# Two dense layers over pairs of token blocks: eight weight groups run upwards and downwards in turn

## The chip, the cores and the metric

One core of one Trainium2 chip runs the whole program in one launch. The metric is the device time of that launch in microseconds (us); a kernel's time is the median of several runs. A profiled execution is one more run, with its own time.

## The reference, cut to what matters

```python
qn = q / (norm(q, axis=1) + 1e-6); kn = k / (norm(k, axis=1) + 1e-6)
a = softmax(kn.T @ qn / tau)                # 256 x 256
x = v @ a                                   # 6016 tokens x 256
h = x @ w_in;  g = h * clip(h + 3, 0, 6) / 6;  x = g @ w_out      # first layer, 256 -> 2048 -> 256
h = maximum(x @ w_in2, 0);  out = (h * h) @ w_out2                # second layer, the same sizes
```

All in float32. The softmax over channels comes first and is short; the kernel multiplies its result into `w_in`, so that the first layer starts from `v` itself.

## The kernel before, in words

Everything is held with channels on the 128 partitions and tokens along the free dimension. Every float32 operand of a product is split into a high and a low part, and each product of two operands is three matmuls (high by high, low by high, high by low).

*Pairs and groups.* The 6016 tokens are cut into six pairs of blocks: five pairs of 2 x 512 tokens and one of 2 x 448 (`pairs`, `NP` = 6). The 2048 hidden channels are cut into eight groups of 256 (`NG` = 8). The list `groups` says in which order the work goes: layer, then pair, then group, groups 0 to 7 in each pair, 96 entries in all. The loop at line 2026 walks over it; `i` is the place in the list and `k = i - K0` the place within the second layer (`K0` = 48). I call the place of a group within its pair its *position*; before the change position and group number are the same.

*A group of the second layer* (`first7s`, `second_of`). A pair of blocks and a group form a 2 x 2 by 2 x 2 block product, which is done with seven products instead of eight. The seven products of the first matrix go through two PSUM banks, X and Y (tile xy, lines 1659 to 1661); ACT copies a bank out (L1671), VectorE adds (L1677), ACT squares or applies the ReLU (L1684), and the split into high (ACT, L1690) and low (VectorE, L1695) follows. The four blocks of a group stand in the tile pairs named rs, rp, hs and rc in turn: groups 0 and 4 in rs, 1 and 5 in rp, 2 and 6 in hs, 3 and 7 in rc. The second matrix takes seven products as well (lines 1802 to 1804, into acc, B, C and xy), three of which need sums of the blocks. These sums are made by DMA: a *move* is an accumulating DMA from SBUF to SBUF that POOL issues (L1711). Each group has two: the first adds one tile to two others (512 KB, `chain`), the second, which waits for the first, adds one to one (256 KB, `chain4`). Three groups later (`LAG`) TensorE uses what they made; ACT and VectorE split it before (`split_t`).

*Weights.* The first matrix of a group, with its sums already formed, lies in DRAM (`w1_d`) and is loaded by SP in two halves of 448 KB (L595, tile w, three buffers `WB` in a ring), two groups ahead (`load_w1(*groups[i + 2])`). In the second layer the first half of group `i + 2` waits until the first move of group `k - 2` has landed, and the second half until its second move has. The second matrix stays in SBUF.

*Other transfers on SP's queue.* SP issues in program order. The tokens of the next pair come in four parts of 256 KB (L817, tile xr), one for each group from position 0 on; with the fifth step of the generator `tokens` the differences of the tokens and their splits are put in (L836 and on). The four results of a pair (`finish_a` at position 0, `finish_b` at position 2 of the next pair) are put into a list `pending`, from which one store is issued per group (L1898).

*What sets the order.* TensorE and the DMA queues take their work in program order. For VectorE, ACT and POOL a planner (`Plan`) takes the operations by due times from a list of costs, tries this 200 times with shifted ranks and emits the best order. So a change in what is asked for, or in when, can change the order of all three engines at other places too.

The lines that the change touches: `w1_tile`, `load_w1`, `fold` and `fold2` (buffers of the weights), `second` (first and last group of an accumulation), `groups`, `by7` and `fast`, `first7s` (choice of the tile pair) and the main loop.

Of the kernel before, what the change touches and what calls it, by code (L numbers as in the profile page):

```python
# [19 lines left out]
P = 128  # L20
# [176 lines left out]
def tile_kernel(  # L197
# [59 lines left out]
    SOME = ()  # L257
    GAP = 2

    PSUM = bass.MemoryType.PSUM  # L260
# [8 lines left out]
    op8_p = ctx.enter_context(tc.tile_pool(name="op8", bufs=2))  # L269
    w1_p = ctx.enter_context(tc.tile_pool(name="w1", bufs=WB))  # L270
    dram = ctx.enter_context(tc.tile_pool(name="dram", bufs=1, space=bass.MemoryType.DRAM))
# [258 lines left out]


    OPW = {"a21": 0, "a11": 1, "a22": 2, "a12": 3, "s1": 4, "s2": 5, "s3": 6, "s4": 7}
    op8_r, w1_r = Ring(2), Ring(WB)
    w1, w1_done, w1_held = {}, {}, {}
# [32 lines left out]

    def w1_tile():
        return pools["w1"].tile([P, 2, 7, P], F32R, tag="w1", name="w1")

# [12 lines left out]
    def load_w1(l, pr, g):  # L583
        p = {}
        a, b = (0, 4) if plain(l, pr) else (1, 8)

        w1[l, pr, g] = p
        free = w1_r.take()
        w1_done[l, pr, g], w1_held[l, pr, g] = [], w1_r.last

        def part(h, waits=()):
            def f():
                if not h:
                    p["w"] = w1_tile()
                o.ins = nc.sync.dma_start(p["w"][:, h, : b - a].bitcast(F32), w1_d[l, g][:, h, a:b])  # L595
                for x in waits:
                    tc.add_manual_dep(
                        o.ins.ins, x.ins.ins.name,
                        mybir.DependencyInfo(mybir.DependencyClass.Sync, mybir.DependencyReason.DATA),
                        reason="order",  # L600
                    )

            o = add("DMA", 0.15 * (b - a), f, free, list(w1_stored[l, g]), *waits, lat=1.5)
            w1_done[l, pr, g].append(o)

        return part
# [6 lines left out]
    def fold(g):  # L613
# [8 lines left out]
        taken, op8_held = op8_r.take(), op8_r.last  # L622
        w1_taken, held = w1_r.take(), w1_r.last
        w1[0, 0, g], w1_done[0, 0, g], w1_held[0, 0, g] = w, [], held
# [8 lines left out]
        for k, es in enumerate(halves):  # L633
# [27 lines left out]
            def place(a=a, b=b):  # L661
                if a == 0:
                    w["w"] = w1_tile()
                return w["w"][:, 0, a:b], w["w"][:, 1, a:b]
# [17 lines left out]
    def fold2(fb):  # L682
# [3 lines left out]
        ts, ws = [{}, {}], [{}, {}]  # L686
        taken, op8_held, w1_taken, held, evs = [], [], [], [], [[], []]
        for k, g in enumerate(gs):
            taken.append(op8_r.take())
            op8_held.append(op8_r.last)  # L690
        for k, g in enumerate(gs):
            w1_taken.append(w1_r.take())
            held.append(w1_r.last)
            w1[0, 0, g], w1_done[0, 0, g], w1_held[0, 0, g] = ws[k], [], held[k]
# [27 lines left out]
        for k, g in enumerate(gs):  # L722

            def place(k=k):
                ws[k]["w"] = w1_tile()
                return ws[k]["w"][:, 0, 0:4], ws[k]["w"][:, 1, 0:4]

            p, ops = split_w(ts[k], 0, 4, place, evs[k], op8_held[k], w1_taken[k])
            w1_done[0, 0, g].extend(ops)

            def f_st(k=k, g=g):
                nc.sync.dma_start(a_d[g], ts[k]["op8"][:, 0:4])

            def store(k=k, g=g, p=p, ops=ops, f_st=f_st):
                a_stored[g] = add("DMA", 0.73, f_st, evs[k], lat=1.5)
                op8_held[k].append(a_stored[g])
                held[k].append(store_w1(0, g, 0, 4, p, ops))

            stores.append(store)
# [672 lines left out]
    def second(l, pr, g, out):  # L1412

        n = pairs[pr][1]
        for k, (b, i) in enumerate(TILES):
            t, half, gh, gl, held = out[k]
            first_of, last_of_b = g == 0 and k in (0, 2), g == NG - 1 and k in (1, 3)
            free = [acc_r[b, e].take() for e in range(NC)] if first_of else [(), ()]
# [82 lines left out]

    groups = [(l, pr, g) for l in range(2) for pr in range(NP) for g in range(NG)]
    K0 = groups.index(FIRST)
    LAG = 3

    def by7(l, pr, g):
        if groups.index((l, pr, g)) < K0:
            return False
        return g in SOME if l == 0 else pr < NP - 1 or g < NG - 2

    def fast(l, pr):
        return groups.index((l, pr, 0)) >= K0

# [128 lines left out]
    def first7s(l, pr, g):  # L1642
# [3 lines left out]
        seven = by7(l, pr, g)  # L1646
        A2, B2 = cells["R"][g % 4]
        R = A2.part + B2.part
# [377 lines left out]
    for i, (l, pr, g) in enumerate(groups):  # L2026
# [13 lines left out]
        elif i >= len(groups) - 2 and us[k - 2]["seven"]:  # L2040
            us[k - 2]["chain4"]()
        for _ in range(1 if k >= 0 else len(pending)):
            if pending and len(us) - pending[0][0] >= HOLD:
# [7 lines left out]
        if l == 0 and pr == 0:  # L2051
            if g + 1 < NG:
# [3 lines left out]
                if g % 2 == 1 and g + 3 < NG:  # L2056
                    need_win((g + 3) // 2)
        if g == (0 if l else 2) and i + NG < len(groups):
            x_load = tokens(*groups[i + NG][:2], k >= 0)
            if k < 0:  # L2060
                list(x_load)
        if k >= 0 and i + NG < len(groups):
            next(x_load, None)
        if k == -5:
# [9 lines left out]
        if k >= 0:  # L2074
# [31 lines left out]
            if k + 1 in due:  # L2106
                us[due[k + 1]]["split_t"]()
            if k and g == 0:
                finish_a(NP * l + pr - 1)
            if k >= NG and g == 2:  # L2110
                finish_b(NP * l + pr - 1)
# [72 lines left out]
```

## Time and profile before

| | |
|---|---|
| median of 3 runs | 1027.7 us (1026.87 to 1028.27) |
| profiled execution | 1026.52 us, of which the span from the first to the last instruction is 1024.7 |
| TensorE busy | 1006.7 us, 98% of the span |
| VectorE, ACT, POOL busy | 908.3, 796.3, 139.4 us |
| mean granted clock of TensorE | 0.998 |
| bytes moved | 199.24 MB |

In the profile PE is TensorE's matmul, PEld its weight load (a little ahead of PE), DVE VectorE, ACT ScalarE, POOL GpSimd, SP the engine that issues most DMAs (SPq its queue). "<-" in a wait names what ended it; `x2` counts merged instructions, and then the duration reaches from the first to the end of the last, with what lies between. The granted clock is in parts of full speed (1.00 is 2.4 GHz, 0.50 is 1.2). The first layer's matmuls end at about 548 us; the second layer runs from there to the end.

### The profile page before, as it was taken

The page shows a single profiled execution, that of the slowest core. Times are in us where ns is not written, and L with a number is a line of the kernel's source. Part 1 is how long each engine was busy: PE and PEld are TensorE (multiplying, and loading weights), DVE is VectorE, ACT ScalarE, POOL GpSimd, SP SyncE. Part 2 cuts the span into 40 slices and gives each one's busy share as a digit, 9 for nine tenths or more (in the row PEclk, how much of TensorE's full clock was granted, in tenths as well). Part 3 has the DMA queues.
Part 4 walks back from the last instruction along what each step waited for, and adds up shares of the span by engine and source line. Part 5 has one row for each costly group of instructions (what it writes and reads, how often), then busy time and mean ns, then how long its engine had stood idle before and what let it go on. Part 6 is the DMA issues. An engine that isn't in the chain of part 4 may idle for free.

```text
span 1024.7 us, 13075 instructions
## 1 busy us (share of the span) xinstructions
PE 1006.7 (98%) x4484; PEld 838.6 (82%) x4484; DVE 908.3 (89%) x1388; ACT 796.3 (78%) x1213; POOL 139.4 (14%) x153
## 2 busy tenths in 40 slices
PE   9999999999999999999999989999999999998998
PEld 8888888888888888888998868788888778787897
DVE  4899988888999999999899979998998888897886
ACT  6787667677778678778768879889889779787884
POOL 4300010000000000010000211222222212122221
PEclk9999999999999999999999999999999999999999
DMA  9657527545445556555764977978989878797883
GB/s 373 253 175 246 180 105 249 176 143 181 151 182 171 195 177 198 185 185 157 263 207 161 231 171 181 219 192 209 226 196 210 202 178 190 176 232 156 204 216 76
DMA packets 73075, 199.24 MB, mean 194 GB/s; under 512 B 7728, under 2 KB 12080, under 8 KB 71856
## 3 DMA queue, kind: packets, MB, share of 16 engines
q1 hardware_dynamic: 49872, 146.63, 43.2%
q0 software_dynamic: 22848, 51.32, 24.5%
q8 instruction: 35, 0.57, 0.2%
q10 hardware_dynamic: 288, 0.46, 0.1%
q14 instruction: 32, 0.26, 0.1%
HBM read 128.45 MB, written 34.34 MB: 159 GB/s over the span
## 4 chain that ended last, share of the span: by engine, by line
PE 67%; DMA 16%; issue 7%; DVE 5%; ACT 3%; POOL 2%; SPq 0%; DVEq 0%; POOLq 0%; ACTq 0%
PE acc L1430 8%; PE acc L1429 8%; PE acc L1435 8%; DMA rs<-rs 6%; DMA hs<-hs 3%; PE xy L1659 3%; PE A L1336 3%; PE A L1337 3%; PE A L1338 3%; PE xy L1661 3%; PE xy L1660 3%; DMA qk<-in_qk_dram 3%; DMA rc<-rc 3%; DMA rp<-rp 2%; PE B L1338 2%
## 5 line engine op out<-in xcount | busy, mean ns | idle before, releaser
L1429 PE MATMUL acc<-g,wo 128*128 128x512 f32 (+1 forms) x384 | 148.2, 386 | 0.0
L1430 PE MATMUL acc<-g,wo 128*128 128x512 f32 (+1 forms) x384 | 148.2, 386 | 0.0
L1218 ACT ACTIVATE g<-r 128x1024 fp32r<-128x1024 f32 (+1 forms) x96 | 100.1, 1043 | 48.2 <-DVE r L1192 47.9
L1222 DVE TENSOR_TENSOR g<-r,g 128x1024 fp32r<-128x1024 f32 (+1 forms) x96 | 115.4, 1202 | 12.0 <-ACT g L1218 11.9
L1435 PE MATMUL acc<-g,wo 128*128 128x512 f32 (+1 forms) x384 | 116.9, 386 | 0.0
L1659 PE MATMUL xy<-xt,w 128*128 128x512 f32 (+1 forms) x192 | 76.0, 396 | 8.7 <-ACT hs L1671 6.0
L1435 PEld LDWEIGHTS acc<-g,wo 128*128 128x128 f32 x384 | 72.1, 188 | 13.8
L1429 PEld LDWEIGHTS acc<-g,wo 128*128 128x128 f32 x384 | 72.1, 188 | 13.7
L1430 PEld LDWEIGHTS acc<-g,wo 128*128 128x128 f32 x384 | 72.1, 188 | 13.6
L1661 PE MATMUL xy<-xt,w 128*128 128x512 f32 (+1 forms) x192 | 74.5, 388 | 0.0
L1660 PE MATMUL xy<-xt,w 128*128 128x512 f32 (+1 forms) x192 | 74.4, 388 | 0.0
L1187 ACT ACTIVATE r<-hp,three 128x1024 f32<-128x1024 f32 (+1 forms) x40 | 45.3, 1132 | 34.8 <-DVE hp L1369 34.4
L1695 DVE TENSOR_TENSOR gs<-rs,gs 128x512 fp32r<-128x512 f32 (+3 forms) x60 | 52.5, 883 | 11.2 <-ACT gs L1690 11.1
L1690 ACT ACTIVATE gs<-rs 128x512 fp32r<-128x512 f32 (+3 forms) x60 | 47.0, 786 | 16.5 <-DMA rs<-rs 15.3
L1659 PE MATMUL xy<-xb,w 128*128 128x512 f32 (+1 forms) x144 | 56.7, 393 | 1.8 <-ACT hs L1684 0.7
L1695 DVE TENSOR_TENSOR gs<-hs,gs 128x512 fp32r<-128x512 f32 (+3 forms) x58 | 50.9, 884 | 6.8 <-ACT gs L1690 6.7
L1802 PE MATMUL acc<-gs,wo 128*128 128x512 f32 (+1 forms) x146 | 56.4, 386 | 0.0
L1804 PE MATMUL acc<-gs,wo 128*128 128x512 f32 (+1 forms) x146 | 56.3, 386 | 0.0
L1803 PE MATMUL acc<-gs,wo 128*128 128x512 f32 (+1 forms) x146 | 56.3, 385 | 0.0
L1661 PE MATMUL xy<-xb,w 128*128 128x512 f32 (+1 forms) x144 | 55.6, 386 | 0.0
L1660 PE MATMUL xy<-xb,w 128*128 128x512 f32 (+1 forms) x144 | 55.6, 386 | 0.0
L1695 DVE TENSOR_TENSOR gs<-rp,gs 128x512 fp32r<-128x512 f32 (+3 forms) x60 | 52.9, 882 | 1.9 <-ACT gs L1690 1.7
(393 smaller groups left out, 2850.4 us busy)
## 6 DMA issues: line engine op xcount, KB each, us to landing
w<-w1d SPq DMA_DIRECT2D x176, 448.0 KB, 4.5
qk<-in_qk_dram SPq DMA_DIRECT2D x8, 1024.0 KB, 14.8
w1d<-wA POOLq DMA_DIRECT2D x16, 448.0 KB, 3.8
xr<-in_vT_dram SPq DMA_DIRECT2D x5, 1024.0 KB, 7.4
x2d<-o SPq DMA_DIRECT2D x20, 256.0 KB, 5.0
rs<-rs POOLq DMA_DIRECT2D x10, 512.0 KB, 8.3
rp<-rp POOLq DMA_DIRECT2D x10, 512.0 KB, 6.5
hs<-hs POOLq DMA_DIRECT2D x10, 512.0 KB, 6.5
```

Source lines behind the costliest of these rows:

```text
L1218: A.activation(t["g"][:, a:b, 0, :n], t["t"][:, a:b, :n], AF.Copy)
L1222: V.tensor_tensor(g[:, a:b, 1, :n], t["t"][:, a:b, :n], g[:, a:b, 0, :n].bitcast(F32), ALU.subtract)
L1429: T_.matmul(acc[b, e][:, :n], w(e, 0), gh_, start=first_of, stop=False)
L1430: T_.matmul(acc[b, e][:, :n], w(e, 1), gh_, start=False, stop=False)
L1435: T_.matmul(acc[b, e][:, :n], w(e, 0), gl_, start=False, stop=last_of_b)
L1659: T_.matmul(ps, wh, xh, start=start, stop=False, skip_group_check=True)
L1660: T_.matmul(ps, wl, xh, start=False, stop=False, skip_group_check=True)
L1661: T_.matmul(ps, wh, xl, start=False, stop=True, skip_group_check=True)
L1695: V.tensor_tensor(lo, src.ap()[..., :n], h.bitcast(F32), ALU.subtract)
L1802: T_.matmul(ps, wh, gh, start=first, stop=False, skip_group_check=True)
L1803: T_.matmul(ps, wl, gh, start=False, stop=False, skip_group_check=True)
L1804: T_.matmul(ps, wh, gl, start=False, stop=last, skip_group_check=True)
```

## The change

1. `groups` runs the eight groups of a pair downwards in some pairs: in the first layer in pairs 2 and 4, in the second in pairs 1, 3 and 5.
2. Each weight buffer has a name of its own, and `Slots` decides ahead of time which group lies in which of the three. A group whose weights are still there is *kept*: `load_w1` then issues nothing. So the first three groups of a pair that turns back are not loaded: four times in the first layer and five times in the second.
3. In the second layer the stores in `pending` are issued at positions 2, 5, 6 and 7 (`POPS`), one each, from the layer's second pair on; in its first pair all that are ready are issued at once. The four token parts come at positions 0 (two), 1 and 2, and the differences with the step at position 3 (`PARTS`).
4. What was said by group number (first and last of an accumulation, tile pair, the ends of a pair) is now said by position.

```diff
+    POPS = {2: 1, 5: 1, 6: 1, 7: 1}
+    PARTS = {0: 2, 1: 1, 2: 1, 3: 1}
...
-    w1_p = ctx.enter_context(tc.tile_pool(name="w1", bufs=WB))
+    w1_p = ctx.enter_context(tc.tile_pool(name="w1", bufs=1))
...
+    groups = []
+    for l in range(2):
+        for pr in range(NP):
+            back = pr % 2 if l else pr > 1 and pr % 2 == 0
+            groups += [(l, pr, g) for g in (reversed(range(NG)) if back else range(NG))]
+    K0 = groups.index(FIRST)
+    at_of = {key: i % NG for i, key in enumerate(groups)}
+
+    class Slots:
+        def __init__(self):
+            now, used = [None] * WB, [-WB + i for i in range(WB)]
+            self.of, self.kept = {}, set()
+            for i, (l, pr, g) in enumerate(groups):
+                what = (l, g, l == 0 and pr < PLAIN)
+                if what in now:
+                    self.kept.add((l, pr, g))
+                    k = now.index(what)
+                else:
+                    k = used.index(min(used))
+                now[k], used[k] = what, i
+                self.of[l, pr, g] = k
+            self.held, self.has = [[] for _ in range(WB)], [None] * WB
+
+        def take(self, key):
+            k = self.of[key]
+            free, self.held[k], self.has[k] = self.held[k], [], key
+            return free, self.held[k], k
...
     def load_w1(l, pr, g):
-        p = {}
+        p, key = {}, (l, pr, g)
         a, b = (0, 4) if plain(l, pr) else (1, 8)
-
-        w1[l, pr, g] = p
-        free = w1_r.take()
-        w1_done[l, pr, g], w1_held[l, pr, g] = [], w1_r.last
+        if key in w1_s.kept:
+            was = w1_s.has[w1_s.of[key]]
+            w1_s.has[w1_s.of[key]] = key
+            for of in w1, w1_done, w1_held:
+                of[key] = of[was]
+            return lambda *_: None
+
+        w1[key] = p
+        free, held, slot = w1_s.take(key)
+        w1_done[key], w1_held[key] = [], held
...
-            first_of, last_of_b = g == 0 and k in (0, 2), g == NG - 1 and k in (1, 3)
+            at = at_of[l, pr, g]
+            first_of, last_of_b = at == 0 and k in (0, 2), at == NG - 1 and k in (1, 3)
...
-    groups = [(l, pr, g) for l in range(2) for pr in range(NP) for g in range(NG)]
-    K0 = groups.index(FIRST)
...
-        return g in SOME if l == 0 else pr < NP - 1 or g < NG - 2
+        return g in SOME if l == 0 else (l, pr, g) not in groups[-2:]
...
-        A2, B2 = cells["R"][g % 4]
+        A2, B2 = cells["R"][at_of[l, pr, g] % 4]
...
-        for _ in range(1 if k >= 0 else len(pending)):
+        pos = i % NG
+        for _ in range(POPS.get(pos, 0) if k >= NG else len(pending)):
             if pending and len(us) - pending[0][0] >= HOLD:
                 pending.pop(0)[1]()
...
-        if g == (0 if l else 2) and i + NG < len(groups):
+        if pos == (0 if l else 2) and i + NG < len(groups):
...
         if k >= 0 and i + NG < len(groups):
-            next(x_load, None)
+            for _ in range(PARTS.get(pos, 0)):
+                next(x_load, None)
...
-            if k and g == 0:
+            if k and pos == 0:
                 finish_a(NP * l + pr - 1)
-            if k >= NG and g == 2:
+            if k >= NG and pos == 2:
                 finish_b(NP * l + pr - 1)
```

The change moves instructions at other places too, through the planner. TensorE's rows are the same in the same order, but for line numbers. Three places, where "group" counts positions within the pair:

POOL, pair 1 of the second layer, the moves of groups 2 (hs), 3 (rc) and of group 4 (rs); 128x2x512 is a group's first move, 128x512 its second. Before:

```order
L1711 DMA hs_5109<-hs_5122 128x2x512
L1711 DMA hs_5122<-hs_5109 128x512
L1711 DMA rc_5186<-rc_5204 128x2x512
L1711 DMA rc_5204<-rc_5186 128x512
L1711 DMA rs_4950<-rs_4975 128x2x512
L1711 DMA rs_4975<-rs_4950 128x512
```

The same moves after the change:

```order
L1746 DMA hs_5062<-hs_5075 128x2x512
L1746 DMA rc_5139<-rc_5157 128x2x512
L1746 DMA hs_5075<-hs_5062 128x512
L1746 DMA rc_5157<-rc_5139 128x512
L1746 DMA rs_4905<-rs_4924 128x2x512
L1746 DMA rs_4924<-rs_4905 128x512
```

The second move of hs has gone behind the first of rc. It stands so at groups 2 and 3 of pairs 0, 3, 4 and 5 before, and of all six pairs after; at groups 0 and 1 of pairs 0, 2, 3 and 4 before, and of pairs 2, 3 and 4 after (and of groups 4 and 5 of pair 5 only before).

SP, pair 3 of the second layer; w is a group's two halves (x2), xr a part of the next pair's tokens, out_dram a store. Positions 0 to 5 before:

```order
L595 DMA w_6803<-w1d_119 128x896 x2
L817 DMA xr_6861<-x2d_137 128x512
L595 DMA w_6878<-w1d_120 128x896 x2
L817 DMA xr_6861<-x2d_137 128x512
L595 DMA w_6960<-w1d_121 128x896 x2
L1898 DMA out_dram<-c_6849 128x512
L817 DMA xr_6861<-x2d_137 128x512
L595 DMA w_7033<-w1d_122 128x896 x2
L817 DMA xr_6861<-x2d_137 128x512
L595 DMA w_7110<-w1d_123 128x896 x2
L1898 DMA out_dram<-c_6863 128x512
L595 DMA w_7178<-w1d_124 128x896 x2
```

Positions 0 to 7 after, where the pair runs downwards:

```order
L853 DMA xr_6737<-x2d_137 128x512 x2
L631 DMA w_6816<-w1d_121 128x896 x2
L853 DMA xr_6737<-x2d_137 128x512
L631 DMA w_6898<-w1d_120 128x896 x2
L1933 DMA out_dram<-c_6790 128x512
L853 DMA xr_6737<-x2d_137 128x512
L631 DMA w_6971<-w1d_119 128x896 x2
L631 DMA w_7048<-w1d_118 128x896 x2
L631 DMA w_7109<-w1d_117 128x896 x2
L1933 DMA out_dram<-c_6801 128x512
L1933 DMA out_dram<-c_6917 128x512
L1933 DMA out_dram<-c_6951 128x512
```

At position 0 the weights have gone and two token parts stand there; the token part of position 3 and the store of position 4 have gone from their places; at positions 6 and 7, where before two groups of weights and two stores follow, only stores are left.

VectorE, pair 3, group 3 and the beginning of group 4; c is a result of the pair before, xt the first difference of the next pair's tokens (xr), f a running sum. Before:

```order
L1677 ISA rc<-xy,rc 128x512
L1923 TENSOR_TENSOR c_6863<-c_6863,f_5104 128x512
L1839 TENSOR_TENSOR f_5712<-xy,f_5712 128x512
L1695 TENSOR_TENSOR gs<-rc,gs 128x512
L1767 TENSOR_TENSOR rc<-rc 128x512
L1677 ISA rs<-xy,rs 128x512
L1695 TENSOR_TENSOR gs<-rc,gs 128x2x512
L1695 TENSOR_TENSOR gs<-rp,gs 128x512
L1695 TENSOR_TENSOR gs<-rc,gs 128x512
L1677 ISA rs<-xy,rs 128x512 x2
L1695 TENSOR_TENSOR gs<-hs,gs 128x2x512
L836 TENSOR_TENSOR xt_7127<-xr_6861 128x512
```

After:

```order
L1712 ISA rc<-xy,rc 128x512
L872 TENSOR_TENSOR xt_6995<-xr_6737 128x512
L1874 TENSOR_TENSOR f_5668<-xy,f_5668 128x512
L1730 TENSOR_TENSOR gs<-rc,gs 128x512
L1802 TENSOR_TENSOR rc<-rc 128x512
L1712 ISA rs<-xy,rs 128x512
```

The difference xt stands ten rows earlier, in the place of c; that row of c stands near the end of group 5 now.

## Rows read from the trace of the kernel before

**Rows 1.** Windows, first layer: us, busy us (instructions) by engine, clock, DMA.

```profile
75.00:525.00 450.00, 450.00 (x2007) 376.54 (x2006) 413.89 (x645) 334.19 (x475) 21.81 (x39) 1.00 0.55 187
```

**Rows 2.** Windows, the six pairs of the second layer, columns as in rows 1.

```profile
546.40:624.50 78.10, 74.70 (x323) 59.30 (x323) 67.71 (x107) 65.06 (x105) 13.80 (x13) 1.00 0.76 188
624.50:702.00 77.50, 77.27 (x337) 62.60 (x336) 69.95 (x99) 66.42 (x104) 17.00 (x16) 1.00 0.85 204
702.00:778.30 76.30, 76.30 (x337) 62.77 (x336) 70.40 (x101) 66.17 (x106) 16.93 (x16) 1.00 0.88 207
778.30:859.30 81.00, 77.66 (x337) 62.48 (x336) 70.02 (x100) 66.23 (x105) 16.79 (x16) 1.00 0.82 195
859.30:941.90 82.60, 79.02 (x338) 63.44 (x337) 69.87 (x100) 66.22 (x106) 16.81 (x16) 0.98 0.81 190
941.90:1011.00 69.10, 69.10 (x337) 62.98 (x336) 58.41 (x89) 58.76 (x100) 15.61 (x15) 1.00 0.81 184
```

**Rows 3.** Waits of PEld, pair 0 (546.4 to 624.5): total us, times, longest.

```profile
PEld xy L1659 <- ACT rp L1671: 2.4, 2, 2.0
PEld xy L1659 <- ACT hs L1671: 1.5, 1, 1.5
```

**Rows 4.** Waits of PEld, pair 3 (778.3 to 859.3).

```profile
PEld xy L1659 <- ACT hs L1671: 2.6, 2, 2.4
PEld xy L1659 <- ACT rp L1671: 1.1, 1, 1.1
PEld xy L1659 <- ACT hs L1684: 1.0, 1, 1.0
```

**Rows 5.** Timeline of ACT, pair 4 group 6: start, us, instruction, [idle before].

```profile
925.21 1.06 ACT L1690 ACTIVATE gs<-rs 128x1024 fp32r<-128x1024 f32 x1 [3.31 <-DMA rs<-rs]
926.17 0.58 ACT L1671 ACTIVATE hs<-xy 128x512 f32<-128x512 f32 x1
```

**Rows 6.** Timeline of PE at that place, then a window with its clock.

```profile
926.80 0.79 PE L1659 MATMUL xy<-xt,w 128*128 128x512 f32 x1 [2.82 <-ACT hs L1671]
...
926.80:929.50 2.70, 2.70 (x6) 2.15 (x7) 2.70 (x5) 1.45 (x3) 0.34 (x1) 0.50 0.90 213
```

**Rows 7.** Timeline of POOL, pair 4: moves of groups 3, 2 and 4.

```profile
904.99 1.19 POOL L1711 DMA_DIRECT2D rc<-rc  x1 [5.62 <-DVE gs L1695]
905.72 1.38 POOL L1711 DMA_DIRECT2D hs<-hs  x1
...
914.70 1.22 POOL L1711 DMA_DIRECT2D rs<-rs  x1 [2.55 <-DVE gs L1695]
```

**Rows 8.** DMA issues: group 4 in pairs 4, 1, 2, then 0 in 3, 1.

```profile
rs<-rs POOLq DMA_DIRECT2D x1, 512.0 KB, 10.4
...
rs<-rs POOLq DMA_DIRECT2D x1, 512.0 KB, 8.0
...
rs<-rs POOLq DMA_DIRECT2D x1, 512.0 KB, 7.1
...
rs<-rs POOLq DMA_DIRECT2D x1, 512.0 KB, 8.9
...
rs<-rs POOLq DMA_DIRECT2D x1, 512.0 KB, 6.9
```

**Rows 9.** Timeline of SP's queue, pair 4, position 5.

```profile
912.70 0.60 SPq L1898 DMA_DIRECT2D out_dram<-c  x1
913.41 2.21 SPq L595 DMA_DIRECT2D w<-w1d  x2
915.67 0.43 SPq L1898 DMA_DIRECT2D out_dram<-c  x1
```

**Rows 10.** Pair 3, groups 2 to 4: SP, that issue's landing, DVE.

```profile
812.54 0.43 SPq L817 DMA_DIRECT2D xr<-x2d  x1
...
xr<-x2d SPq DMA_DIRECT2D x1, 256.0 KB, 5.6
...
818.03 0.69 DVE L1839 TENSOR_TENSOR f<-xy,f 128x512 f32<-128x512 f32 x1 [0.79 <-PE xy L1804]
```

More of the change, by code (lines that the diff above doesn't have):

```diff
@@ L528, in load_wo2 @@
         wo_done[1, i] = add("DMA", 1.46, f, wo2_stored[i], wo_held[0, i], lat=1.5)
+    groups = []
[23 more added lines that the diff above has]
+            return free, self.held[k], k
     OPW = {"a21": 0, "a11": 1, "a22": 2, "a12": 3, "s1": 4, "s2": 5, "s3": 6, "s4": 7}
-    op8_r, w1_r = Ring(2), Ring(WB)
+    op8_r, w1_s = Ring(2), Slots()
     w1, w1_done, w1_held = {}, {}, {}
@@ L566, in split_w, with w1_tile @@
         return p, [hi, lo]
-    def w1_tile():
-        return pools["w1"].tile([P, 2, 7, P], F32R, tag="w1", name="w1")
+    def w1_tile(k):
+        return pools["w1"].tile([P, 2, 7, P], F32R, tag=f"w1{k}", name="w1")
     def store_w1(l, g, a, b, p, ops, queue=None):
@@ L593, in f @@
                 if not h:
-                    p["w"] = w1_tile()
+                    p["w"] = w1_tile(slot)
                 o.ins = nc.sync.dma_start(p["w"][:, h, : b - a].bitcast(F32), w1_d[l, g][:, h, a:b])
@@ L622, in fold @@
         taken, op8_held = op8_r.take(), op8_r.last
-        w1_taken, held = w1_r.take(), w1_r.last
+        w1_taken, held, slot = w1_s.take((0, 0, g))
         w1[0, 0, g], w1_done[0, 0, g], w1_held[0, 0, g] = w, [], held
@@ L662, in place @@
                 if a == 0:
-                    w["w"] = w1_tile()
+                    w["w"] = w1_tile(slot)
                 return w["w"][:, 0, a:b], w["w"][:, 1, a:b]
@@ L686, in fold2 @@
         ts, ws = [{}, {}], [{}, {}]
-        taken, op8_held, w1_taken, held, evs = [], [], [], [], [[], []]
+        taken, op8_held, w1_taken, held, slots, evs = [], [], [], [], [], [[], []]
         for k, g in enumerate(gs):
@@ L691, in fold2 @@
         for k, g in enumerate(gs):
-            w1_taken.append(w1_r.take())
-            held.append(w1_r.last)
+            for x, y in zip((w1_taken, held, slots), w1_s.take((0, 0, g))):
+                x.append(y)
             w1[0, 0, g], w1_done[0, 0, g], w1_held[0, 0, g] = ws[k], [], held[k]
@@ L724, in place @@
             def place(k=k):
-                ws[k]["w"] = w1_tile()
+                ws[k]["w"] = w1_tile(slots[k])
                 return ws[k]["w"][:, 0, 0:4], ws[k]["w"][:, 1, 0:4]
@@ L1508, in by7 @@
             return False
-        return g in SOME if l == 0 else pr < NP - 1 or g < NG - 2
+        return g in SOME if l == 0 else (l, pr, g) not in groups[-2:]
     def fast(l, pr):
-        return groups.index((l, pr, 0)) >= K0
+        return groups.index((l, pr, 0)) >= K0 - (K0 % NG)
     class Cell:
```

## The prediction

> **What bounds the kernel now.** TensorE does, and the question is only where it stands still. I read the busy time of stretches first. From 75 to 525 us, nearly all of the first layer, TensorE is busy for all of 450.00 us [rows 1]: there is nothing to win there, however many transfers go. The second layer, cut at the starts of its pairs of blocks, takes 78.1, 77.5, 76.3, 81.0 and 82.6 us for its five pairs of 512 tokens [rows 2]. Pairs 1 to 4 hold the same work, and in pair 2 TensorE is busy for all of the 76.30 us [rows 2], so that is the floor. Against it pair 1 loses 1.2, pair 3 4.7 and pair 4 6.3 us. Pair 0 holds somewhat less work, so its loss is read from its waits: 2.4 + 1.5 = 3.9 us [rows 3]. Together 16.1 us are lost that a change in the second layer could give back; pair 5, of 448 tokens, has TensorE busy throughout [rows 2] and is left as it is.
>
> Next, who is late. TensorE waits for ACT in nearly all of it; in pair 3 that is 2.6 us for the copies at L1671 into hs, 1.1 into rp, and 1.0 for L1684 [rows 4]. ACT is not busy then: it waits for a DMA. The clearest place is group 6 of pair 4. ACT stands for 3.31 us in front of the split of rs (L1690) until the move of group 4 into rs has landed, at 925.21; the copy that TensorE needs comes behind it, at 926.17 [rows 5]. TensorE starts again at 926.80 after 2.82 us, and then for 2.7 us at a granted clock of 0.50, the lower of its two levels [rows 6], which is another 1.3 us. That move was issued by POOL at 914.70 [rows 7] and took 10.4 us. The same move took 8.0 us in pair 1 and 7.1 in pair 2 [rows 8], where TensorE lost nothing at this place. ACT reached the split at 925.21 - 3.31 = 921.90, 7.2 us after the issue: up to 7.2 us the move costs nothing.
>
> Why 10.4? Around it SP issues, from 912.70 to 916, a store of 256 KB, two halves of weights of 448 KB (128 x 896 float32) and a second store [rows 9]. They come in a heap because each half waits until a move has landed, and because POOL has the second move of group 2 (hs, 905.72) behind the first of group 3 (rc, 904.99) [rows 7]: transfers that would have been spread wait for that late landing in SP's queue and then leave together.
>
> **The change, part by part.** *Loads that go.* The order of SP has 27 groups of weights fewer, 54 transfers of 448 KB, 12 groups of them in the first layer, where [rows 1] makes them worth 0. In the second layer they go at positions 6, 7 and 0 of pairs. TensorE's weight loads show no wait for weights in these pairs, so nothing comes back directly. TensorE loses its time at positions 2, 3, 5 and 6, where five of eight loads remain. What helps is that the moves of groups 5 to 7 run alone and land earlier, and with them the next pair's first halves go out before the move of group 0 rather than with it. That move took 8.9 us in pair 3, where a half and a token part went out together with it, and 6.9 in pair 1, where the half was ahead of it [rows 8]. I take 6.9 for all pairs. ACT waits for it at position 2; L1684 behind it cost TensorE 1.0 us in pair 3 [rows 4]. With 2.0 us less I leave 0.4 us per pair for positions 2 and 3 together with the small waits there, pair 1's loss at that place being of this size; the bounds are 0 and 1.4.
>
> *Stores and token parts.* The store of position 4 goes to 5, and the token part of position 3 to 0. The new store of position 5 needs the difference c12 of line 1957, which VectorE now has near the end of group 5, so it goes out behind the move of group 4. Two stores of 256 KB and no weights fall out of the heap around that move. I take 8.0 us for it, pair 1's row, beside which fewer transfers left; bounds 7.1 (pair 2) and 10.4 [rows 8]. At 8.0 ACT waits 0.8 us instead of 3.31. TensorE's wait was 0.5 shorter than ACT's, so 0.3 to 0.6 us per pair are left, and I take 0.6; the lower clock, which came only after the 2.82 us, does not come.
>
> By the Trainium skill, page "DMA: Bandwidth & Descriptors", section "Queues, rings and completion order", each DMA engine alternates between its queue rows packet by packet; so POOL's move would get its turn beside SP's row however much is queued there, and only a row that runs empty during the move would shorten it. By that rule the weights still queued would keep the move near 10 us, and the sum would be that of the third rival below. The trace leaves this open: 8.0 against 10.4 us goes with the amount beside it, but in pair 1 SP's row may just have run empty.
>
> *Order of the moves.* This speaks against the change. Before, the second move of group 2 stood behind the first of group 3 in pairs 0, 3, 4 and 5, and not in pairs 1 and 2, the two that lose little. Now it does so in all six pairs (the POOL rows above show pair 1). The heap in front of group 4's move so comes to pairs 1 and 2 too, and ACT's order there is now that of pair 3. So I give pairs 1 to 4 the same rest: 0.4 at positions 2 and 3, 0.2 for the late move of hs (1.1 in pair 3 [rows 4], none in pair 4), 0.6 at position 6, 0.3 for the small waits for f: 1.5 us each. Pair 0 keeps its weights up to position 5. There the third copy of group 6 now stands ahead of the split, so of its 3.9 us I take the 1.5 as gone and 0.6 as added for what else moves: 3.0, bounds 1.5 and 3.9.
>
> *A new wait.* The first difference of the next tokens (L836, now L872) moves on VectorE from group 4 into group 3, to the slot where c12 was formed, and it needs the fourth token part. In pair 3 that part (then the third) was issued at 812.54 and took 5.6 us, so it landed at 818.1; the work behind the slot, the addition into f, began at 818.03 after 0.79 us idle [rows 10]. With 0.69 us for the difference itself, VectorE would come out about 0.75 us late, and the addition into f, the sum for the next move and POOL's move of group 3 wait behind it. With group 0's move landing 2 us sooner the part lands sooner too, and the price is 0. Bounds 0 and 0.75 per pair in four pairs; I take 0.
>
> *The rest.* TensorE's own order is the same row for row. The slots hand out buffers two groups ahead as before. The stores of x2d that pair 0 now issues at once, and the last two groups, whose order is unchanged on TensorE, I put at 0, with 0.3 us either way.
>
> **The sum.** Before: 3.9 + 1.2 + 0 + 4.7 + 6.3 = 16.1 us. After: 3.0 + 4 x 1.5 = 9.0. The gain is 7.1 us. The profiled execution took 1026.5 us (a span of 1024.7 and 1.8 around it), so the changed one would take 1019.4; the median of the runs lies 1.2 us above the profiled one, which makes 1020.6.
>
> **The rivals.**
> *Slower: the heap spreads.* If the move of group 4 keeps taking 9 us and more, all of pairs 1 to 4 lose what pair 3 loses, 4.7 us: 3.0 + 18.8 = 21.8, that is 5.7 us more than before, 1033.4 us. It decides at the landing 7.2 us after the issue, and grows with every us beyond. For it speaks POOL's order, and that weights at positions 1 to 5 stay; against it that the two stores leave the heap.
> *The new wait.* 0.75 us in each of four pairs: 9.0 + 3.0 = 12.0, a gain of 4.1, 1023.6 us. It needs the fourth part to land as late as before.
> *No change: the move is shared, not queued.* The move of group 4 stays near 10 us, and only positions 2 and 3 gain: position 6 leaves 2.4 in place of 0.6, so 3.0 + 4 x 3.3 = 16.2 us against 16.1: 1027.8 us.
> *All of it.* Every move under 7.2 us, as in pair 2: pair 0 at 1.5 and 0.2 for each other, 2.3 us, a gain of 13.8: 1013.9 us. Pair 2 shows that it can be, with all its weights loaded [rows 2].
> That the loads do not go is excluded by SP's order.
>
> **How the numbers follow.** The forecast has 0.44, the full gain 0.15, the new wait 0.11, no change 0.14, slower 0.16. Some 0.2%, 2 us, is what a measurement of this kernel can tell from no change. So faster is 0.44 + 0.15 + 0.11 = 0.70, same 0.14, slower 0.16. The range reaches from the full gain, 1013, over the case of no change with 1 us for the tail and the run, 1029, and leaves out the slower case.
>
> **What would show it.** Right: pairs 1 to 4 of the second layer at 77 to 78.5 us each; group 0's move near 7 and group 4's near 8 us from issue to landing; no stretch at a clock of 0.50 in the second layer; position 6, 7 and 0 moves near 5 us. Wrong: pairs 1 and 2 at 80 us and ACT in front of the split of rs for over 2 us in each pair (the slower rival); VectorE idle in front of the first token difference in group 3 (the new wait); group 4's move at 10 us though both stores come later (shared, not queued). A wait of TensorE in the first layer, or for weights kept from the pair before, would be outside of all that I reckoned with.

## The result, and the profile after

The changed kernel takes 1017.54 us (median of four runs, 1017.25 to 1018.2) against 1027.99 us for the kernel before on the same chip (1026.87 to 1028.6): a ratio of 0.9901, 95% interval 0.9883 to 0.9918. It is faster by 1.0%, and 3.1 us below the forecast. The span of the profiled execution fell from 1024.7 to 1015.9 us.

Windows of the trace after: the first layer's stretch, then pairs 0 to 4 of the second layer (length, then busy us of PE, PEld, DVE, ACT, POOL, granted clock, DMA share, GB/s).

```profile
75.00:525.00 450.00, 450.00 (x2010) 377.14 (x2009) 414.38 (x650) 334.82 (x476) 22.33 (x40) 1.00 0.48 163
...
545.91:620.16 74.25, 73.95 (x323) 59.35 (x321) 69.92 (x113) 65.27 (x105) 13.88 (x13) 1.00 0.74 183
620.16:697.69 77.53, 77.36 (x337) 62.58 (x336) 70.28 (x100) 66.25 (x105) 16.92 (x16) 1.00 0.72 165
697.69:775.45 77.76, 77.08 (x337) 62.51 (x336) 70.02 (x100) 66.29 (x105) 16.81 (x16) 1.00 0.74 168
775.45:853.89 78.44, 77.19 (x337) 62.65 (x336) 69.82 (x100) 66.29 (x105) 16.78 (x16) 1.00 0.72 166
853.89:931.75 77.86, 77.02 (x337) 62.59 (x336) 69.42 (x100) 66.31 (x106) 16.84 (x16) 1.00 0.72 166
```

Against [rows 2]: the first layer is as full as in [rows 1] although the DMA engines have less to do there (0.48 for 0.55). Pairs 0, 3 and 4 are shorter by 3.8, 2.6 and 4.7 us, pair 1 is equal, and pair 2 is *longer* by 1.45. No pair has a stretch at the lower clock any more.

Pair 4, positions 2 to 5, on POOL and on SP's queue, the counterparts of [rows 7] and [rows 9], and the landing of group 4's move, the counterpart of the first line of [rows 8]:

```profile
899.35 1.19 POOL L1746 DMA_DIRECT2D rc<-rc  x1 [5.82 <-DVE gs L1730]
900.08 1.38 POOL L1746 DMA_DIRECT2D hs<-hs  x1
905.35 0.86 POOL L1746 DMA_DIRECT2D rc<-rc  x1 [3.89 <-DMA rc<-rc]
908.93 1.22 POOL L1746 DMA_DIRECT2D rs<-rs  x1 [2.72 <-DVE gs L1730]
```

```profile
906.39 3.12 SPq L631 DMA_DIRECT2D w<-w1d  x3
...
912.66 1.99 SPq L1933 DMA_DIRECT2D out_dram<-c  x3
```

```profile
rs<-rs POOLq DMA_DIRECT2D x1, 512.0 KB, 7.3
```

POOL's order is still inverted here (hs second behind rc first), and three halves of weights still leave in a heap from 906.39 on. But the stores (three of them) come 3.7 us behind the move's issue and not on both sides of it, and the move takes 7.3 us instead of 10.4.

The waits in the second layer before the last pair (total us, times, longest). TensorE's largest is now for the running sums f of VectorE; in [rows 3] and [rows 4] it was for ACT's copies.

```profile
DVE xt L872 <- DMA xr<-x2d: 4.7, 3, 1.9
PEld xy L1694 <- DVE f L1874: 4.5, 9, 1.2
PEld xy L1694 <- ACT rp L1706: 1.6, 3, 0.9
```

### The profile page after: what moved, and what is told of

Read it like the earlier page. It is cut to its first block, busy times and chain, and to the rows that moved or that the text cites. A ratio compares the mean times of both kernels' runs of the same rounds, so it can differ in the third digit from the quotient of the medians.

```text
span 1015.9 us, 12955 instructions
## 1 busy us (share of the span) xinstructions
PE 1005.5 (99%) x4484; PEld 838.6 (83%) x4484; DVE 905.8 (89%) x1388; ACT 796.2 (78%) x1213; POOL 139.5 (14%) x153
## 4 chain that ended last, share of the span: by engine, by line
PE 81%; DMA 8%; issue 5%; DVE 4%; ACT 1%; POOL 1%; SPq 0%; DVEq 0%; POOLq 0%
PE acc L1472 8%; PE acc L1466 8%; PE acc L1467 8%; PE xy L1694 5%; PE xy L1696 5%; PE xy L1695 5%; PE A L1374 4%; PE A L1372 4%; PE A L1373 4%; DMA rs<-rs 3%; PE s L1004 3%; PE acc L1837 3%; PE acc L1838 3%; PE acc L1839 3%; PE B L1372 2%
## 5 line engine op out<-in xcount | busy, mean ns | idle before, releaser
L1694 PE MATMUL xy<-xt,w 128*128 128x512 f32 (+1 forms) x192 | 75.3, 392 | 1.4 <-ACT rc L1706 0.8
L1695 PE MATMUL xy<-xt,w 128*128 128x512 f32 (+1 forms) x192 | 74.2, 386 | 0.0
L1696 PE MATMUL xy<-xt,w 128*128 128x512 f32 (+1 forms) x192 | 74.2, 386 | 0.0
L1228 DVE SCALAR_TENSOR_TENSOR r<-r,hp 128x1024 f32<-128x1024 f32 (+1 forms) x40 | 47.9, 1196 | 9.9 <-ACT r L1223 9.6
```

The lines of the kernel that those rows point to most:

```text
L1694: T_.matmul(ps, wh, xh, start=start, stop=False, skip_group_check=True)
L1695: T_.matmul(ps, wl, xh, start=False, stop=False, skip_group_check=True)
L1696: T_.matmul(ps, wh, xl, start=False, stop=True, skip_group_check=True)
```

## The experiments

A source edit lets the planner reorder three engines, so all experiments hold the order of VectorE, ScalarE and GpSimd to a list, that of the changed kernel or that of the kernel before, and change one thing besides. Each ratio is against runs of the kernel before on the same chip. The table gives the lengths of pairs 0 to 4 in the profiled execution. Between executions a pair that an edit doesn't touch differs by up to some 1.3 us (pair 4 has 77.86 in the changed kernel and 76.56 in the one with pair 0 inverted, where only pair 0 is edited), so single small differences carry nothing.

| kernel | median us | ratio (95%) | pairs 0 to 4, us |
|---|---|---|---|
| before | 1025.41 to 1027.99 | 1 | 78.0, 77.5, 76.3, 81.0, 82.5 |
| changed | 1017.54 | 0.9901 (0.9883 to 0.9918) | 74.3, 77.5, 77.8, 78.4, 77.9 |
| before's order, loads gone only | 1028.32 | 1.0019 (1.0000 to 1.0038) | 78.2, 78.8, 78.6, 81.5, 79.2 |
| changed, all weights loaded | 1017.73 | 0.9920 (0.9896 to 0.9945) | 74.4, 76.7, 77.3, 78.0, 78.2 |
| changed, stores in the heap | 1031.09 | 1.0050 (1.0023 to 1.0078) | 75.3, 79.0, 83.1, 81.8, 79.7 |
| changed, moves in turn | 1012.50 | 0.9862 (0.9838 to 0.9885) | 73.7, 77.4, 76.7, 76.6, 76.5 |
| before's order, stores only | 1022.89 | 0.9976 (0.9955 to 0.9996) | 77.6, 77.6, 77.6, 79.9, 79.3 |
| changed, four parts at 0 | 1016.03 | 0.9890 (0.9860 to 0.9920) | 75.9, 76.5, 76.9, 77.4, 78.1 |
| changed, pair 0 inverted | 1021.06 | 0.9929 (0.9902 to 0.9955) | 77.3, 77.5, 78.3, 79.0, 76.6 |
| before, moves in turn | 1014.31 | 0.9876 (0.9849 to 0.9904) | 73.7, 77.6, 77.1, 77.9, 77.3 |
| changed, in turn, four parts at 0 | 1013.35 | 0.9868 (0.9836 to 0.9900) | 73.6, 76.6, 76.5, 76.6, 76.6 |
| changed, in turn, stores in the heap | 1014.11 | 0.9869 (0.9834 to 0.9904) | 73.7, 77.4, 76.5, 76.9, 76.5 |
| before, in turn, stores moved | 1014.05 | 0.9868 (0.9832 to 0.9903) | 73.8, 76.8, 77.6, 76.7, 76.5 |
| changed, in turn, all weights loaded | 1014.60 | 0.9875 (0.9838 to 0.9911) | 74.2, 76.7, 77.3, 76.6, 76.5 |

### Loads gone alone, and all else without it

The changed kernel with before's order, stores and token parts (its groups still turn back and its first three are kept):

```diff
-        for _ in range(POPS.get(pos, 0) if k >= NG else len(pending)):
+        for _ in range(1 if k >= 0 else len(pending)):
...
-    PARTS = {0: 2, 1: 1, 2: 1, 3: 1}
+    PARTS = {i: 1 for i in range(8)}
```

> The kernel before with the groups run upwards and downwards and the kept weights not loaded, and nothing else: stores and token parts stand at their old positions, and VectorE, ACT and POOL keep the kernel before's order row for row. Theory (the heap): the losses come from what SP's queue lets go beside the moves of groups 0 and 4, at positions 1 to 5 where the weights stay, so little changes: group 4's move stays at 9 us or more in pairs 3 and 4 of the second layer, pair 1 to 4 together go from 317.4 us to no less than 313, and the time is 1023 to 1027 us. Rival (the traffic): 25 MB less makes every move shorter, group 4's move goes to about 7 us and the time to 1016 to 1020 us, most of the gain.

And the changed kernel, in its own order, with every group's weights loaded:

```diff
-                what = (l, g, l == 0 and pr < PLAIN)
+                what = (l, pr, g)
```

> The changed kernel with every group's weights loaded (nothing kept); stores, token parts and the order of VectorE, ACT and POOL as changed, row for row. Theory (the heap): stores and order made the gain, so most of it stays: group 4's move at 7 to 8 us, pairs 1 to 4 at 78 to 79.5 us each, 1018 to 1023 us. Rival (the traffic): the moves are as long as before the change, and the time is 1026 us or more.

The first gives 1.0019 (1028.32 us, a little above the 1023 to 1027 of the theory; pairs 1 to 4 together 318.1 us), the second 0.9920, the same as the changed kernel within the intervals. Some 25 MB less to move are worth nothing measurable; what gains is in the stores, the token parts and the engines' order.

### Stores put back beside group 4's move

The changed kernel, in its own order, with its stores of positions 5 to 7 at positions 4 to 6 and c12 the last of them:

```diff
-    POPS = {2: 1, 5: 1, 6: 1, 7: 1}
+    POPS = {2: 1, 4: 1, 5: 1, 6: 1}
...
-        out_s(pr, 0, 0, S["c12"].ap, c12, S["c12h"])
...
         out_s(pr, 1, 1, c21.ap, o, held)
+        out_s(pr, 0, 0, S["c12"].ap, c12, S["c12h"])
```

> The changed kernel with the last three stores of a pair in the order c22, c21, c12 and at positions 4, 5 and 6, so that two stores of 256 KB leave again just ahead of and beside group 4's move, as they did before the change; the order of all engines but SP is unchanged. Theory (the heap): that move goes from about 7.2 back to 9 to 10 us, ACT stands about 2 us in front of its split, pairs 1 to 4 lose 1.5 to 2.5 us each, 1023 to 1028 us. Rival (the DMA engines share by queue, so that the amount queued on SP does not count): the move stays under 8 us and the time at 1017 to 1019 us.

Measured 1.0050: slower than the kernel before, and more so than the 1023 to 1028 us of the theory, with pairs 2 and 3 at 83.1 and 81.8 us. In these two the granted clock is at 0.50 again for some 3.4 us behind the wait at position 6 (from 768.6 and 850.5), which is part of the excess. Group 4's move took 8.8, 10.3, 9.5 and 10.6 us in pairs 1 to 4, where it had taken 7.1, 7.3, 6.9 and 7.3. Pair 3 there, on POOL, on SP's queue, the landing of group 4's move, and ACT and PE behind it:

```profile
819.69 1.22 POOL L1752 DMA_DIRECT2D hs<-hs  x1 [4.71 <-DVE gs L1736]
827.58 1.20 POOL L1752 DMA_DIRECT2D rc<-rc  x1 [6.67 <-DVE gs L1736]
828.31 1.39 POOL L1752 DMA_DIRECT2D hs<-hs  x1
...
838.01 1.21 POOL L1752 DMA_DIRECT2D rs<-rs  x1 [4.07 <-DVE gs L1736]
```

```profile
816.64 19.28 SPq L637 DMA_DIRECT2D w<-w1d  x4
836.01 0.39 SPq L1939 DMA_DIRECT2D out_dram<-c  x1
836.50 0.89 SPq L637 DMA_DIRECT2D w<-w1d  x2
837.48 0.44 SPq L1939 DMA_DIRECT2D out_dram<-c  x1
```

```profile
rs<-rs POOLq DMA_DIRECT2D x1, 512.0 KB, 9.5
```

```profile
847.63 1.06 ACT L1731 ACTIVATE gs<-rs 128x1024 fp32r<-128x1024 f32 x1 [2.58 <-DMA rs<-rs]
...
849.23 0.50 PE L1700 MATMUL xy<-xt,w 128*128 128x512 f32 x1 [2.10 <-ACT hs L1712]
```

This is [rows 5, 6 and 9] again. The last of the four halves leaves only at 835.6 (the row ends at 816.64 + 19.28 = 835.92): it waits for the second move of hs, issued at 828.31. A store, two more halves and a store, which were queued behind it, then leave within 2 us, and group 4's move goes out right behind them. ACT stands 2.58 us, TensorE 2.10. So the stores beside group 4's move do matter in this order, and the slower rival's way is real: it gave 1033.4, this kernel 1031.1.

### Moves strictly in turn

The same kernel as the changed one but for POOL's list, in which a group's second move stands ahead of the next group's first wherever it stood behind it:

```diff
 hs first (128x2x512)
-rc first (128x2x512)
 hs second (128x512)
+rc first (128x2x512)
 rc second (128x512)
```

> The changed kernel with POOL's moves strictly in turn, the second of a group always ahead of the first of the next; all other engines as changed. Theory (the heap, charged to the order of the moves in the prediction): the halves of weights are let go one after the other, hs's second move lands 2 us and more earlier at position 4, group 4's move takes 6 to 7 us, pairs 1 to 4 come to 76.5 to 77.3 us and the time to 1012 to 1015 us. Rival: the first move of groups 1 and 3 is held back behind the landing of the one before, by up to 2 us, and its splits come late; 1018 us or more.

Measured 1012.50 us (1012.09 to 1013.94), ratio 0.9862: better than every run of the changed kernel, and on the same chip than every run of the changed kernel with all weights loaded (1016.33 and more). Windows of its pairs 2 to 4:

```profile
697.59:774.25 76.66, 76.61 (x338) 62.69 (x337) 69.99 (x100) 66.04 (x105) 17.02 (x16) 1.00 0.75 170
774.25:850.86 76.61, 76.61 (x338) 62.72 (x336) 70.02 (x100) 66.07 (x105) 16.95 (x16) 1.00 0.73 170
850.86:927.35 76.49, 76.49 (x338) 62.72 (x337) 69.45 (x100) 66.27 (x106) 16.97 (x16) 1.00 0.74 169
```

They stand within 0.4 us of the floor of [rows 2]; group 4's move takes 5.2 to 6.0 us. VectorE's wait for the tokens is gone from the waits too.

The same edit on the kernel before, with nothing else changed:

> The kernel before, its operations held in their old order, with one edit: GpSimd's moves stand strictly in turn, first and second move of a group before the next group's first. Theory (a second move behind the next group's first is what makes group 4's and group 0's late): pair 0 falls by 3 us, pair 3 by 3.5, pair 4 by 5, group 4's move to 7 us or less, median 1015 to 1019. Rival (stores beside the moves decide alone): group 4's move stays at 9.7 us or more in pairs 3 and 4, no change, ratio 0.998 or more.

Ratio 0.9876: the old kernel with its moves in turn has a span of 1012.0 us, 12.7 less, with no load kept and no store moved. Pair 4 falls from 82.5 to 77.3 and group 4's move there from 10.4 to 6.4 us. Only in pair 1, where no move was inverted, it stays long, 8.5 us, and position 6 takes 9.67 us all the same. The rival falls.

### The stores alone

The kernel before in its own order, with the stores at the changed kernel's positions:

```diff
-        for _ in range(1 if k >= 0 else len(pending)):
+        for _ in range(POPS.get(g, 0) if k >= NG else 1 if k >= 0 else len(pending)):
```

> The kernel before, its operations on VectorE, ScalarE and GpSimd held in their old order; only the places of the stores change, from pair 1 on: positions 2, 5, 6 and 7 of a pair, pair 0 as before. Theory of the heap (stores beside group 4's move cost it its time): group 4's move falls from 9.7 to 10.4 us to 7 to 7.5 in pairs 3 and 4, these two pairs fall by 2 to 3.5 us each, the others move by 0.5 at most; 4 to 6 us in all, ratio 0.994 to 0.996. Rival (the gain came with the other order of the engines' work): ratio 0.999 or more.

Ratio 0.9976, about half of the gain expected: group 4's move fell only from 9.4 and 10.4 to 8.4 and 8.6 us in pairs 3 and 4 (the 9.7 of the expectation is the time until the next move's issue). Neither side of the expectation held. The stores are a part. The rest of the changed kernel's gain came with the order that the planner found or with the new places of the token parts; no run moved these alone in the old order.

### Do the stores matter with the moves in turn?

The "stores in the heap" edit once more, now with the moves in turn:

> The changed kernel with the stores beside group 4's move as in the run of stores in the heap (c22, c21 and c12 at positions 4, 5 and 6), and GpSimd's moves strictly in turn. Theory (a second move behind the next group's first is what makes the heap harmful; the stores alone are not): group 4's move 7 us or less, pairs 1 to 4 within 77.5 us each, median 1011 to 1015. Rival (the stores beside group 4's move cost by themselves): group 4's move 8.5 or more, pairs of 79 to 83 us, 1022 or more.

Ratio 0.9869, against 1.0050 with the moves inverted: the same stores at the same places cost 1.5% against the changed kernel in one order and nothing against its 0.9862 with the moves in turn, within the intervals, in the other. Pair 3 again, to be laid beside the rows above:

```profile
813.24 1.22 POOL L1752 DMA_DIRECT2D hs<-hs  x1 [2.34 <-DVE gs L1736]
819.04 0.92 POOL L1752 DMA_DIRECT2D hs<-hs  x1 [4.59 <-DMA hs<-hs]
820.37 1.20 POOL L1752 DMA_DIRECT2D rc<-rc  x1 [0.41 <-DVE gs L1736]
...
829.94 1.21 POOL L1752 DMA_DIRECT2D rs<-rs  x1 [2.25 <-DVE gs L1736]
```

```profile
809.74 14.57 SPq L637 DMA_DIRECT2D w<-w1d  x4
824.41 0.93 SPq L1939 DMA_DIRECT2D out_dram<-c  x1
826.54 6.68 SPq L637 DMA_DIRECT2D w<-w1d  x2
833.32 0.65 SPq L1939 DMA_DIRECT2D out_dram<-c  x1
```

```profile
rs<-rs POOLq DMA_DIRECT2D x1, 512.0 KB, 5.5
```

The second move of hs is issued 5.8 us after the first, not 8.6: the first took 5.5 us and not 6.7, and POOL does not stand for VectorE's sums for rc ahead of the second. It lands 10.7 us after the first was issued, not 15.9 (it took 4.9 us and not 7.3), so the fourth half leaves at 824, the store at 824.41 and the next half at 826.54, all before group 4's move at 829.94. The heap doesn't form; what is put in SP's row there no longer counts.

The stores moved in the kernel before with its moves in turn, and the loads put back in the changed kernel with its moves in turn:

> The kernel before with its old order, GpSimd's moves strictly in turn and the stores at positions 2, 5, 6 and 7 from pair 1 on. Theory (with the moves in turn the places of the stores decide nothing): within 2 us of the run with the moves in turn alone, 1012 to 1016. Rival (stores and moves add up): another 2.5 us off as in the run of the stores alone, 1010 to 1012.

> The changed kernel with GpSimd's moves strictly in turn and all weights loaded, none kept. Theory (the loads gone are worth nothing, as in the run of the changed kernel with all loads): 1011 to 1013.5. Rival (they were hidden behind the late moves and count now that these are gone): 1015 or more.

0.9868 and 0.9875: neither the places of the stores nor the kept weights add anything that can be told to the moves in turn. With all weights loaded the median, 1014.60, lies between the theory's 1013.5 and the rival's 1015, and the interval (0.9838 to 0.9911) leaves room for some us either way.

### Pair 0, and the fourth token part

The changed kernel with the moves of groups 0 and 1 in pair 0 inverted as before:

```diff
 rs first (128x2x512)
-rs second (128x512)
 rp first (128x2x512)
+rs second (128x512)
 rp second (128x512)
```

> The changed kernel with the moves of pair 0's groups 0 and 1 on GpSimd in the inverted order that the kernel before has. Theory (pair 0 gained because the inversion went there): pair 0 goes back from 74.25 to 76.5 to 78 us, median 1020 to 1021.5. Rival (pair 0 gained by the places of its stores and of the tokens' load): pair 0 stays within 0.5 us, median 1018 or less.

Pair 0 goes from 74.25 to 77.30 us, the median to 1021.06. The same moves after, and then in this kernel:

```profile
561.00 1.25 POOL L1746 DMA_DIRECT2D rs<-rs  x1 [62.25 <-DVE gs L1730]
567.41 0.92 POOL L1746 DMA_DIRECT2D rs<-rs  x1 [5.15 <-DMA rs<-rs]
569.76 1.19 POOL L1746 DMA_DIRECT2D rp<-rp  x1 [1.43 <-DVE hs L1712]
```

```profile
562.35 1.25 POOL L1752 DMA_DIRECT2D rs<-rs  x1 [61.89 <-DVE gs L1736]
571.20 1.21 POOL L1752 DMA_DIRECT2D rp<-rp  x1 [7.60 <-DVE hs L1718]
571.98 1.34 POOL L1752 DMA_DIRECT2D rs<-rs  x1
```

One pair of exchanged rows on an engine that is busy for 14% of the span is worth 3 us. The loss shows at groups 3 to 5 here and showed at groups 5 and 6 before, so it isn't the same wait each time. Over all runs pair 0 takes 77.3 to 78.2 us in the four kernels with this inversion and 73.6 to 75.9 in the ten without it.

All four parts at position 0:

```diff
-    PARTS = {0: 2, 1: 1, 2: 1, 3: 1}
+    PARTS = {0: 4, 3: 1}
```

> The changed kernel with all four parts of the tokens' load at position 0 of a pair in place of one at position 3. Theory (the fourth part comes late for the transposition xt, and f waits for that): VectorE's waits for the load fall from 4.7 us to nothing, TensorE's waits for f from 4.5 to 2 or less, median 1014.5 to 1016. Rival (parts beside group 7's and group 0's moves delay these): 1017.5 or more.

VectorE's wait for the load is gone and TensorE's for f falls from 4.5 to 1.3 us, and pairs 1 to 4 together from 311.6 to 308.9, but pair 0 is 1.6 us longer in this profile. By the median, 0.9890 against 0.9901, nothing is shown. With the moves in turn as well:

> The changed kernel with GpSimd's moves strictly in turn and all four parts of the tokens' load at position 0. Theory (the moves were the loss, the parts at 0 harm nothing): pairs 76.3 to 77.4 us each, median 1011 to 1012.5, ratio 0.984 to 0.987. Rival (the parts at 0 delay group 0's move, which with the moves in turn is next): 1014 or more.

0.9868: all five pairs are at the floor in the profile, yet the median, 1013.35, lies between what the theory and the rival gave and is that of the other kernels with the moves in turn. Which of them is the fastest can't be told. By their medians all six with the moves in turn are ahead of the changed kernel, by 3 to 5 us, but they were not measured beside it and their intervals overlap its own; the first of them, at 1012.50, has the clearest lead.

## Why the prediction was right or wrong

The time was within the range and the sign right. The reasons held in part.

**Group 4's move and position 6: right, a little too dear.** Forecast near 8.0 us, measured 7.1, 7.3, 6.9 and 7.3: about the 7.2 us up to which it was to cost nothing, so position 6 is at 9.55 to 9.65 us against 9.52, where 0.6 us had been left. The prediction's own row had shown that 8.0 us in pair 1 cost nothing; the 7.2 us were pair 4's. The lower clock went with the wait, as said.

**What the Trainium skill's rule was made to say: wrong in its application.** By the Trainium skill, page "DMA: Bandwidth & Descriptors", section "Queues, rings and completion order", a DMA engine takes turns packet by packet between the queue rows that have work; from this the prediction drew that the weights alone would keep the move near 10 us. The move took 7.3 us beside three halves, the first of which left 2.5 us earlier, and 9.5 with two stores among them. The packets in the trace tell more. q0 is the queue of the moves and q1 that of SP; a row gives packets, MB and the share of the 16 DMA engines. Before the change, pair 4, the move issued at 914.70, from 915 to 919 us and then from 919 to 925.2:

```profile
q1 hardware_dynamic: 389, 1.07, 100.9%
```

```profile
q0 software_dynamic: 272, 0.52, 46.0%
q1 hardware_dynamic: 300, 0.72, 32.4%
```

After the change, pair 4, the move issued at 908.93, from 909 to 911.9 us:

```profile
q1 hardware_dynamic: 329, 1.06, 101.4%
```

In each first stretch q0 moves nothing. The move began some 4.3 us behind its issue before and some 3.0 us after the change, while SP's transfers filled the DMA engines; a move by itself began some 1.8 us behind it (group 5 of pair 3 after the change, issued at 842.43). The rest took 6.1, 4.3 and 3.2 us. So the turns of the Trainium skill's rule can at most describe the second stretch, where both queues move packets. What holds the beginning back is not shown, and the amount queued alone does not give the length: with a half and a token part that left 0.3 and 0.7 us behind it (the rows of pair 2 below), the move of group 0 took 8.1 us.

**The order of the moves: seen, but under-read.** The prediction named the inversion as the cause of the heap and charged it alike to pairs 1 to 4. Their sum came out at 311.6 us for 305.2 + 6.0 = 311.2 forecast, and nearly evenly, pair 2's loss included. The split was not as forecast: most of the rest lies at positions 3 to 5 (pair 4's group 3 10.79, pair 3's group 4 10.57, group 5 10.37), little at 6. So the sum came out in part by luck: position 6, put at 0.6 us in each of four pairs, lost next to nothing, and the new wait, put at 0, took about as much (below).

**Pair 0: the mis-sized term.** A gain of 0.9 was taken, with a rest of at least 1.5; measured 3.8, a rest of 0.6 above the 73.65 us that it has with the moves in turn. The inverted moves of groups 0 and 1, which stood there before and not after, are listed with the change, but the step on the order of the moves priced only groups 2 and 3. Putting them back costs 3.05 us. This term alone is 2.9 us too small. The span gained 8.8 us for the 7.1 forecast, since 1.3 were lost again in the last pair and the end (put at 0, with 0.3 either way), 0.4 in pairs 1 to 4, and 0.5 were won before pair 0: 2.9 + 0.5 - 0.4 - 1.3 = 1.7. The 0.5 is scatter: pair 0 starts anywhere from 545.4 to 549.8 us in these profiles. The other 1.4 us of the 3.1 by which the time was missed are the step from the profiled execution to the median: 1.2 us were added for it, and after the change the median lies 0.14 below the profiled execution, 1017.68.

**Loads that go: right that they bring nothing directly, wrong that group 0's move falls to 6.9 us with them.** It took 8.6, 8.1, 7.9 and 7.2 us in pairs 1 to 4 of the changed kernel; with all weights loaded it took 6.7, 6.0, 6.3 and 8.5. In the old order the loads gone shortened it in three pairs and not in pair 2 (5.7, 8.3, 7.7 and 6.2 against 6.9, 5.9, 8.9 and 8.5). Pair 2 on SP's queue, around the move issued at 715.63, and later VectorE's wait:

```profile
715.95 0.32 SPq L631 DMA_DIRECT2D w<-w1d  x1
716.31 0.43 SPq L853 DMA_DIRECT2D xr<-x2d  x1
723.80 7.30 SPq L631 DMA_DIRECT2D w<-w1d  x2
731.20 0.50 SPq L1933 DMA_DIRECT2D out_dram<-c  x1
731.75 0.44 SPq L853 DMA_DIRECT2D xr<-x2d  x1
```

```profile
737.11 0.69 DVE L872 TENSOR_TENSOR xt<-xr 128x512 f32<-128x512 f32 x1 [1.79 <-DMA xr<-x2d]
```

A half and a token part still leave right behind the move. In pair 1 it has a price: in the changed kernel and its four variants with loads gone and parts at positions 0 to 3, where the move took 8.4 to 8.7 us, group 3 has 10.42 to 10.44; in the four where it took 6.7 to 7.1, 9.63 to 9.69.

**The new wait: put at 0, and it came.** The same rows show why. The fourth part left at 731.75, behind a half that waited until 730.8 for the second move of group 0. That move is late mostly because it runs beside the first move of rp, issued ahead of it: it took 6.6 us here and 4.8 with the moves in turn. The prediction let the part wait for the first move alone. VectorE stood 4.7 us in three pairs. TensorE's waits for f right behind these stands are 0.99, 1.16 and 0.31 us, 2.5 in all; the first of them:

```profile
738.45 0.19 PEld L1694 LDWEIGHTS xy<-xb,w 128*128 128x128 f32 x1 [0.99 <-DVE f L1874]
```

With the parts at position 0 the sum of pairs 1 to 4 falls by 2.7 us, of which the sooner move of group 0 in pair 1 is a part, so the price is near 2.5 us and not settled closer.

**The rivals.** All of it, 1013.9 us, was reached by the kernels with the moves in turn (1012.5 to 1014.6), and not by the change. The slower one came with the stores back in the heap.

**What stays open.** That the inversion costs this time is shown by taking it out in both kernels and by putting it in, in pair 0, in the changed one. Whether its price comes through the weights held in SP's row alone or in part through the two moves that share the engines (hs second takes 7.3 us issued behind rc first, 4.9 ahead of it) was not separated: a kernel whose second halves don't wait for second moves was not run.

## What to carry to other kernels

When two queues are tied together by waits, look first for the instruction that stands behind a stranger's wait in an in-order queue: here a 256 KB move behind the next group's first, on an engine busy for 14%, cost more than the 25 MB of loads and the four stores that the change worked on. Before sizing a term from transfers that "collide", ask why they leave together. Where a planner sets orders, count every inversion in every pair and price each, and hold the order to a list before crediting a source edit with a gain.

## What the runs showed of the hardware

The same 512 KB accumulating move from SBUF to SBUF took 5.0 us by itself, 5.5 beside one half of 448 KB issued ahead of it and one 3 us behind, 7.3 with three halves ahead of and beside it and three stores of 256 KB from 3.7 us behind its issue on, 8.1 with a half and a token part of 256 KB issued 0.3 and 0.7 us behind it, and 9.5 with three halves and two stores issued in the 2.5 us ahead of it. Its first packets came some 1.8 us behind its issue when it was alone, and 3.0 and 4.3 us behind it where SP's transfers filled the DMA engines. So its length followed what SP's queue was moving in its first microseconds, by up to a factor of two, and not the amount alone.
